# Linear attention and soft mixture of experts on one core: the phases of the loop put in another order, the first pair and the table setup moved between engines

## Chip, core and metric

The kernel runs on one core of one Trainium2 chip. A core has five engines that run side by side, each in its own program order: TensorE (PE, matrix products and transposes[...]; its weight loads are shown as PEld), VectorE (DVE), ScalarE (ACT), GpSimd (POOL[...]) and SyncE (SP, which here only issues transfers). An engine that meets an instruction whose input is not ready waits, and all that stands behind it in that engine's program waits too. The order of instructions in this kernel is the order in which they are written, engine by engine; the framework adds the semaphores. The metric is the time of one execution on the device, in microseconds (us).

## What is computed

Two steps, one after the other. The first is a linear attention with a decaying state, for 4 batches of 8 heads, 768 positions, head size 48. The second is a soft mixture of 8 experts with 4 slots each, on all 3072 rows of 384.

```python
# r, k, v: [4, 8, 768, 48]   w, u: [8, 48]   phi: [384, 32]   w1: [8, 384, 1024]   w2: [8, 1024, 384]
for t in range(S):
    y[:, :, t] = r_t @ (state + (u * k_t) v_t^T)
    state = w * state + k_t v_t^T
x = y as [3072, 384]
logits = x @ phi
d = softmax of logits over the rows;  slot_input = d.T @ x
for e in range(8):
    slot_out[e] = relu(slot_input[e] @ w1[e]) @ w2[e]
out = softmax of logits over the slots @ slot_out
```

## The kernel before

The sequence is cut into chunks of 128 positions. Two chunks make a pair (256 rows), so there are 12 pairs, three to a batch. For a pair `n` the program has these parts (`P` = 128, `J` = 2 interleaved position sets, `H` = 8 heads, `D` = 48, `nP` = 4 head pairs; `g` is the chunk of the pair):

```python
def mults(n):                       # scale r and k by powers of w; u * k; cast v
    nc.gpsimd.tensor_mul(rr[:, :, :, 0:D], jh(r_l), W_n[:])
    nc.gpsimd.tensor_mul(kk[:, :, :, 0:D], jh(k_l), W_k[:])
    nc.gpsimd.tensor_mul(ku[:], jh(k_l), u_rep[...])
    nc.scalar.copy(v_bf[:], jh(v_l))

def r_copy(n, j):                   # r into PSUM, tile rp (one buffer)
    nc.scalar.copy(s["rp"][:], jh(loads[n][0])[:, j, :, :])
def kur(n, j):
    nc.vector.tensor_mul(ku[:, j], ku[:, j], rp[:])
def diag(n):                        # sum of u*k*r per head, times v: the position's own term
    nc.vector.tensor_reduce(d, ku[:], axis=X, op=add)
    nc.vector.tensor_mul(dv[:], v_bf[:], d[...])

def trans(n, nm):                   # eight transposes into t_p (one buffer), then a copy
    nc.tensor.transpose(t_p[...], ...)          # x8
    nc.scalar.copy(t_s[:], t_p[:])

def att(n, j):                      # 16 matmuls into at_p0, at_p1 (one buffer each), then two masks
    nc.tensor.matmul(at_p[a][...], kT[...], rT[...])
    nc.vector.tensor_mul(s["at"][:, j, a, :, :], at_p[a][:], mask[:, j, None, :])

def y_open(n):    ...               # 4 matmuls: dv into y_p
def inter(n, g):  ...               # 4 matmuls: earlier state times r, into y_p
def state(n, g):                    # new state in PSUM s_p (one buffer), then times w^128
    nc.tensor.matmul(s_p[:], ident[:], st[...])
    nc.tensor.matmul(s_p[...], kk[...], v_bf[...])     # x8
    nc.vector.tensor_mul(st2[...], s_p[:], wm[...])
def intra(n):                       # 32 matmuls: masked attention times v; then x copied to SBUF
    nc.tensor.matmul(y_p[...], at_s[...], v_bf[...])
    nc.scalar.copy(x_t[:], y_p[...])

def xt(n):        ...               # 6 transposes of x, copy on ScalarE (xt_s)
def lg(n):        ...               # 6 matmuls: logits; exponential on ScalarE (Lexp)
def disp(n, s_p): ...               # 8 matmuls: d.T @ x and the column sums; added to un_a on VectorE
def lexp_t(g):                      # every second pair: exponentials transposed, row sums
    nc.tensor.transpose(le_p[...], Lexp, ident);  nc.vector.tensor_copy(LexpT[...], le_p[...])
    nc.tensor.matmul(rs_p, LexpT[...], blk);      nc.vector.reciprocal(rsum_r[...], rs_p)

def tables():                       # w^128 by seven squarings; tables for state and logits
    for _ in range(C.bit_length() - 1):
        nc.vector.tensor_mul(w_pd[:], w_pd[:], w_pd[:])
    for par in range(2):
        nc.vector.tensor_copy(wm[...], w_pd[...])
    nc.vector.tensor_copy(phi_s[:], phi_f[:])
```

The start and the loop call them like this:

```python
mults(0); mults(1)
r_copy(0, 0); kur(0, 0); r_copy(0, 1); kur(0, 1)
trans(0, "rr"); trans(0, "kk")
tables()
diag(0)
for n in range(nS + 2):             # nS = 12; calls for pairs that do not exist do nothing
    load(n + 3)
    disp(n - 2, s_now)
    att(n, 0)
    mults(n + 2)
    trans(n + 1, "rr")
    r_copy(n + 1, 0); kur(n + 1, 0)
    att(n, 1)
    trans(n + 1, "kk")
    r_copy(n + 1, 1); kur(n + 1, 1)
    y_open(n); inter(n, 0); state(n, 0)
    xt(n - 1)
    inter(n, 1); state(n, 1); intra(n)
    lg(n - 1)
    diag(n + 1)
    if 2 <= n and n % 2 == 0: lexp_t(n // 2 - 1)
    load_w(W_AT[n])                 # weights of the experts, issued on GpSimd's queue
```

After the loop the column sums are inverted, the experts run (`up`, `down`), and the output is made from `LexpT` and the slot outputs, in 24 blocks written by 12 transfers.

Of the kernel before, what the change touches and what calls it, by code (L numbers as in the profile page):

```python
# [11 lines left out]
def kernel(  # L12
# [52 lines left out]
    def load(n):  # L65
        if n >= nS:
            return
        b, i = divmod(n, nSb)
        loads[n] = []
        for name, src in (("r_l", r), ("k_l", k), ("v_l", v)):  # L70
            t = ld.tile([P, H, J, D], f32, name=name)
            nc.sync.dma_start(out=t[:].rearrange("p h j d -> p h (j d)"),  # L72
                              in_=src[b, :, i * TS:(i + 1) * TS, :].rearrange("h (p j) d -> p h (j d)", j=J))
            loads[n].append(t)

# [5 lines left out]
    u_rep = cst.tile([P, H, D], f32, name="u_rep")  # L81
    nc.scalar.dma_start(out=u_rep[:].rearrange("p h d -> p (h d)"), in_=u.flatten().partition_broadcast(P))
    for n in range(3):
        load(n)

    w_pd = cst.tile([P, nP], f32, name="w_pd")
    nc.vector.memset(w_pd[:], 1.0)
    warm = cst.tile([P, 1], f32, name="warm")
# [7 lines left out]
    make_identity(nc, ident)  # L96
    for par in range(2):
        nc.gpsimd.dma_start(out=w_pd[par * 64:par * 64 + D, :],
                            in_=w.rearrange("(q a) d -> a d q", a=2)[par])
    phi_f = cst.tile([P, nM, ES], f32, name="phi_f")  # L100
# [11 lines left out]
    nc.vector.tensor_copy(col_f[:], col_i[:])  # L112
    mask = cst.tile([P, J, P], f32, name="mask")
    for j in range(J):
# [30 lines left out]
    st_t = [cst.tile([P, nP, D2], bf, name=f"st{i}") for i in range(2)]  # L145

    def tables():
        for _ in range(C.bit_length() - 1):
            nc.vector.tensor_mul(w_pd[:], w_pd[:], w_pd[:])  # L149
        for par in range(2):  # L150
            sl = slice(par * 64, par * 64 + 64)
            nc.vector.tensor_copy(wm[sl, :, par * D:(par + 1) * D],
                                  w_pd[sl, :, None].to_broadcast([64, nP, D]))
        nc.vector.tensor_copy(phi_s[:], phi_f[:])

# [22 lines left out]
    with tc.tile_pool(name="wk", bufs=2) as wk, \  # L178
# [4 lines left out]
        def mults(n):  # L183
            if n >= nS:
                return
            r_l, k_l, v_l = loads[n]
            rr, kk = rr_t[n % NB], kk_t[n % NB]
            nc.gpsimd.tensor_mul(rr[:, :, :, 0:D], jh(r_l), W_n[:])  # L188
            nc.gpsimd.tensor_mul(kk[:, :, :, 0:D], jh(k_l), W_k[:])  # L189
            ku = wk.tile([P, J, H, D], f32, name="ku")  # L190
            nc.gpsimd.tensor_mul(ku[:], jh(k_l), u_rep[:, None, :, :].to_broadcast([P, J, H, D]))  # L191
            v_bf = wk3.tile([P, J, H, D], bf, name="v_bf")
            nc.scalar.copy(v_bf[:], jh(v_l))
            sc[n] = dict(rr=rr, kk=kk, ku=ku, v=v_bf, at={})

# [37 lines left out]
        def att(n, j):  # L233
            if n >= nS:
                return
            s = sc[n]
            rT, kT = s["t_rr"], s["t_kk"]
            if j == 0:
                s["at"] = wk.tile([P, J, 2, nP, P], bf, name="at_s")
            at_p = [ps.tile([P, nP, P], f32, name=f"at_p{a}") for a in range(2)]  # L240
            for q in range(nP):
                for g in range(2):
                    for a in range(2):
                        sl = slice(a * 64, a * 64 + 64)
                        nc.tensor.matmul(at_p[a][g * HF:(g + 1) * HF, q, :], kT[sl, q, g, j, :],  # L245
                                         rT[sl, q, g, :, :].rearrange("p j c -> p (j c)"),
                                         start=True, stop=True, tile_position=(a * 64, g * HF),
                                         skip_group_check=True)
            for a in range(2):
                nc.vector.tensor_mul(s["at"][:, j, a, :, :], at_p[a][:],  # L250
                                     mask[:, j, None, :].to_broadcast([P, nP, P]))
# [24 lines left out]
        def state(n, g):  # L276
# [4 lines left out]
            first = i == 0 and g == 0  # L281
            if g == 0 and "s" not in s:
                s["s"] = ps.tile([P, nP * D2], f32, name="s_p")
            s_p = s["s"]
            st, st2 = st_t[(2 * n + g) % 2], st_t[(2 * n + g + 1) % 2]
            if not first:
# [3 lines left out]
            for q in range(nP):  # L290
                for j in range(J):
# [4 lines left out]
                                     tile_position=(g * HF, 0), skip_group_check=True)  # L296
            nc.vector.tensor_mul(st2[:].rearrange("p q e -> p (q e)"), s_p[:],  # L297
                                 wm[:].rearrange("p q e -> p (q e)"))
# [3 lines left out]
        def intra(n):  # L302
            s = sc[n]
            for a in range(2):
                for q in range(nP):
                    h = 2 * q + a
                    for j in range(J):
                        for g in range(2):
                            sl = slice(g * HF, (g + 1) * HF)
                            nc.tensor.matmul(s["y"][:, g, h * D:(h + 1) * D], s["at"][sl, j, a, q, :],  # L310
                                             s["v"][sl, j, h, :],
                                             start=False, stop=(a == 1 and q == nP - 1 and j == J - 1),
                                             tile_position=(g * HF, 0), skip_group_check=True)
            x_t = wk3.tile([P, 2, Dm], bf, name="x_t")
            nc.scalar.copy(x_t[:], s["y"][:, :, 0:Dm])  # L315
            x_of[n] = x_t
            del sc[n]
# [15 lines left out]

        le_of = {}

        def lg(n):
            if not 0 <= n < nS:
                return
            xl_p, xt_s = xl_of.pop(n)
            lg_p = xl_p[:, XW:XW + 4 * ES].bitcast(f32)  # L340
            for g in range(2):
                for mi in range(nM):
                    o = (g * nM + mi) * P
                    nc.tensor.matmul(lg_p[:, g * ES:(g + 1) * ES], xt_s[:, o:o + P], phi_s[:, mi, :],
                                     start=(mi == 0), stop=(mi == nM - 1), skip_group_check=True)
            if n % 2 == 0:
                le_of[n // 2] = wk.tile([P, G, ES], bf, name="Lexp")
            nc.scalar.activation(out=le_of[n // 2][:, 2 * (n % 2):2 * (n % 2) + 2, :].rearrange("p g s -> p (g s)"),
                                 in_=lg_p, func=AF.Exp)

        def disp(n, s_p):
# [14 lines left out]
            del x_of[n]  # L366

        def lexp_t(g):
            le_p = ps.tile([P, P + 2 * G], bf, name="le_p", tag="xl_p", padded_shape=[P, XW + 4 * ES])
            nc.tensor.transpose(le_p[:, 0:P], le_of[g][:].rearrange("p g s -> p (g s)"), ident[:])  # L370
            nc.vector.tensor_copy(LexpT[:, g, :].rearrange("s (p j) -> s j p", j=J),
                                  le_p[:, 0:P].rearrange("s (j p) -> s j p", j=J))
            rs_p = le_p[:, P:P + 2 * G].bitcast(f32)
            nc.tensor.matmul(rs_p, LexpT[:, g, :], blk[:], start=True, stop=True, skip_group_check=True)
            nc.vector.reciprocal(rsum_r[:, g * G:(g + 1) * G], rs_p)

        W_AT = [0, 1, 1, 1, 1, 1, 1, 1, 1, 1, 1, 2, 2, 2, 2]
        mults(0)
        mults(1)
        r_copy(0, 0)  # L380
        kur(0, 0)
        r_copy(0, 1)
        kur(0, 1)
        trans(0, "rr")
        trans(0, "kk")
        tables()
        diag(0)
        for n in range(nS + 2):
            live = n < nS
            load(n + 3)  # L390
            if live:
                sc[n]["s"] = ps.tile([P, nP * D2], f32, name="s_p")
                s_now = sc[n]["s"]
            else:
                s_now = ps.tile([P, nP * D2], f32, name="s_p")
            disp(n - 2, s_now)
            att(n, 0)
            mults(n + 2)
            trans(n + 1, "rr")
            r_copy(n + 1, 0)  # L400
            kur(n + 1, 0)
            att(n, 1)
            trans(n + 1, "kk")
            r_copy(n + 1, 1)
            kur(n + 1, 1)
            if live:
                y_open(n)
                inter(n, 0)
                state(n, 0)
            xt(n - 1)  # L410
            if live:
                inter(n, 1)
                state(n, 1)
                intra(n)
            lg(n - 1)
            diag(n + 1)
            if 2 <= n and n % 2 == 0 and n // 2 <= nG:
                lexp_t(n // 2 - 1)
            load_w(W_AT[n])
# [93 lines left out]
```

The softmax here doesn't subtract the row's maximum and nothing guards it: scores larger than these inputs give would overflow.

## Time and profile before

The median of two runs is 176.5 us (175.2 and 177.8); the profiled execution has a span of 173.4 us.

| Engine | busy, us | share of the span | instructions |
|---|---|---|---|
| TensorE, matmuls | 108.8 | 63% | 1927 |
| TensorE, weight loads | 80.3 | 46% | 1927 |
| VectorE | 103.3 | 60% | 205 |
| ScalarE | 74.1 | 43% | 114 |
| GpSimd | 81.2 | 47% | 64 |

| What the loop is made of | engine | count | mean, us |
|---|---|---|---|
| rr, kk, ku products (lines 188, 189, 191) | GpSimd | 12 each | 1.84, 1.81, 1.81 |
| mask products, `at_s` (line 250) | VectorE | 48 | 0.68 |
| `ku` times `rp` (line 208) | VectorE | 24 | 0.55 |
| reduce and `dv` (lines 215, 217) | VectorE | 12 each | 0.95, 0.95 |
| state table `st` (line 297) | VectorE | 20 | 0.56 |
| copies `t_rr`, `t_kk` (line 230) | ScalarE | 12 each | 1.01 |
| copies `xt_s`, `x_t`, cast `v_bf` | ScalarE | 12 each | 0.80, 0.80, 0.83 |
| copy `rp` (line 202) | ScalarE | 24 | 0.49 |

The page of a profile gives the busy time of each engine; then the span in 40 equal slices, each digit being a busy share in tenths (the row PEclk is the granted clock of TensorE in tenths); then the groups of instructions with what ended the idle time before them. A line of the timeline has start, duration (both us), engine, source line, operation, output and inputs, shapes and count, and in brackets the idle time of that engine just ahead, with the instruction that ended it. A line of the windows has the stretch, its length, busy us and number of instructions for PE, PEld, DVE, ACT and POOL, then granted clock, DMA share and GB/s. Busy time of TensorE is modelled at the end of each matmul, since matmuls are pipelined.

### The profile page before, as it was taken

How to read it: one execution, taken by the hardware profiler on the slowest of the kernel's cores; microseconds unless marked ns; L12 is line 12 of the kernel's file. 1: busy time of each engine (PE TensorE's matmuls, PEld its weight loads, DVE VectorE, ACT ScalarE, POOL GpSimd, SP SyncE). 2: the span in 40 equal slices, each digit the busy share in tenths (PEclk: the TensorE clock that was granted, in tenths of full speed). 3: DMA queues.
4: the chain of work that ended last, by engine and by line, in shares of the span. 5: the costliest groups of instructions: out<-in, count | busy, mean ns of one | idle time of the engine just before them, and what ended most of it. 6: DMA issues, size and time to landing. Idle time of an engine off the chain costs nothing.

```text
span 173.4 us, 4471 instructions
## 1 busy us (share of the span) xinstructions
PE 108.8 (63%) x1927; PEld 80.3 (46%) x1927; DVE 103.3 (60%) x205; ACT 74.1 (43%) x114; POOL 81.2 (47%) x64
## 2 busy tenths in 40 slices
PE   0020505679567889598748979797984838978200
PEld 0010403556445566466536756565663628962000
DVE  2062999394895686668775587666766333328510
ACT  3534521265765546547743555463550320008510
POOL 7089948193999085776758096991000000000000
PEclk9999999999995555857985555555576575555555
DMA  5999980559999997989999909299999993005994
GB/s 66 252 278 308 319 241 0 132 144 161 292 145 293 218 262 107 271 143 215 241 242 197 146 4 146 43 166 210 208 207 210 205 206 49 8 4 203 365 363 160
DMA packets 52628, 32.19 MB, mean 186 GB/s; under 512 B 38000, under 2 KB 49520, under 8 KB 52608
## 3 DMA queue, kind: packets, MB, share of 16 engines
q0 software_dynamic: 11616, 12.63, 46.2%
q1 hardware_dynamic: 40848, 19.07, 38.5%
q10 hardware_dynamic: 144, 0.20, 0.9%
q8 instruction: 15, 0.25, 0.5%
q14 instruction: 5, 0.04, 0.1%
HBM read 39.77 MB, written 4.72 MB: 257 GB/s over the span
## 4 chain that ended last, share of the span: by engine, by line
PE 44%; DVE 22%; ACT 14%; DMA 7%; SPq 5%; issue 4%; ACTq 0%; DVEq 0%
PE t_p L227 10%; PE s_p L292 6%; SPq L72 5%; PE at_p L245 4%; DMA out_dram<-o_s 4%; ACT t_rr L230 4%; PE y_p L272 4%; DVE w_pd L149 4%; DVE at_s L250 4%; DVE dv L217 3%; PE xl_p L329 3%; ACT x_t L315 3%; PE so_p L447 3%; DVE rp L215 3%; PE h_p L435 3%
## 5 line engine op out<-in xcount | busy, mean ns | idle before, releaser
L189 POOL TENSOR_TENSOR kk<-k_l,W_k 128x768 bf16<-128x768 f32 x12 | 21.7, 1808 | 27.3 <-PE s_p L292 27.3
L250 DVE TENSOR_TENSOR at_s<-at_p,mask 128x512 bf16<-128x512 f32 x48 | 30.8, 684 | 2.6 <-PE at_p L245 2.4
L245 PE MATMUL at_p<-t_rr,t_kk 64*64 64x128 bf16 x384 | 17.8, 294 | 12.8 <-DVE at_s L250 11.7
L208 DVE TENSOR_TENSOR ku<-ku,rp 128x384 f32<-128x384 f32 x24 | 13.3, 554 | 19.8 <-ACT rp L202 19.6
L188 POOL TENSOR_TENSOR rr<-r_l,W_n 128x768 bf16<-128x768 f32 x12 | 22.1, 1843 | 5.5 <-DVE W_n L125 5.3
L191 POOL TENSOR_TENSOR ku<-k_l,u_rep 128x768 f32<-128x768 f32 x12 | 21.7, 1812 | 2.8 <-DVE rp L215 2.8
L230 ACT COPY t_rr<-t_p 128x1024 bf16<-128x1024 bf16 x12 | 12.1, 1012 | 16.6 <-PE t_p L227 16.5
L245 PEld LDWEIGHTS <-t_kk 64*64 64x64 bf16 x384 | 11.0, 145 | 17.3 <-issue 15.3
L227 PE MATMUL t_p<-ident,rr 128*128 128x128 bf16 x96 | 11.6, 296 | 11.5 <-POOL rr L188 11.5
L297 DVE TENSOR_TENSOR st<-s_p,wm 128x384 bf16<-128x384 f32 x20 | 11.1, 556 | 11.4 <-PE s_p L292 11.4
L230 ACT COPY t_kk<-t_p 128x1024 bf16<-128x1024 bf16 x12 | 12.1, 1012 | 11.8 <-PE t_p L227 11.8
L331 ACT COPY xt_s<-xl_p 128x768 bf16<-128x768 bf16 x12 | 9.6, 800 | 17.0 <-PE xl_p L329 17.0
L227 PE MATMUL t_p<-ident,kk 128*128 128x128 bf16 x96 | 11.4, 294 | 6.1 <-ACT t_rr L230 5.4
L315 ACT CAST x_t<-y_p 128x768 bf16<-128x768 f32 x12 | 9.6, 799 | 13.2 <-PE y_p L310 13.2
L227 PEld LDWEIGHTS <-rr 128*128 128x128 bf16 x96 | 8.6, 135 | 13.2 <-POOL rr L188 11.5
L292 PE MATMUL s_p<-v_bf,kk 64*128 64x96 bf16 x160 | 14.5, 254 | 0.0
L480 ACT ACTIVATE o_s<-o_p,rsum_r 128x384 f32<-128x384 f32 x12 | 6.4, 585 | 18.1 <-PE o_p L474 15.6
L202 ACT COPY rp<-r_l 128x384 f32<-128x384 f32 x24 | 11.7, 488 | 5.1 <-DVE dv L217 4.4
L292 PEld LDWEIGHTS <-kk 64*128 64x128 bf16 x160 | 10.7, 121 | 6.4 <-issue 6.4
L176 POOL DMA_DIRECT2D w_all<-in_moe_w_dram x16 | 13.6, 856 | 0.0
L227 PEld LDWEIGHTS <-kk 128*128 128x128 bf16 x96 | 9.2, 132 | 7.8 <-issue 6.1
L272 PE MATMUL y_p<-st,t_rr 128*128 128x96 bf16 x80 | 8.9, 254 | 5.0 <-DVE st L297 5.0
(76 smaller groups left out, 185.7 us busy)
## 6 DMA issues: line engine op xcount, KB each, us to landing
w_all<-in_moe_w_dram POOLq DMA_DIRECT2D x16, 768.0 KB, 8.5
r_l<-in_r_dram SPq DMA_DIRECT2D x12, 384.0 KB, 4.9
k_l<-in_k_dram SPq DMA_DIRECT2D x12, 384.0 KB, 5.4
v_l<-in_v_dram SPq DMA_DIRECT2D x12, 384.0 KB, 6.4
out_dram<-o_s SPq DMA_DIRECT2D x12, 384.0 KB, 4.2
w_rep<-in_w_dram SPq DMA_DIRECT2D x1, 192.0 KB, 5.5
u_rep<-in_u_dram ACTq DMA_DIRECT2D x1, 192.0 KB, 6.0
phi_f<-in_moe_phi_dram POOLq DMA_DIRECT2D x1, 48.0 KB, 6.4
```

Of the source, the lines that this page charges most:

```text
L176: nc.gpsimd.dma_start(out=dst[:, e, :, :], in_=src[:, e, :, :])
L188: nc.gpsimd.tensor_mul(rr[:, :, :, 0:D], jh(r_l), W_n[:])
L189: nc.gpsimd.tensor_mul(kk[:, :, :, 0:D], jh(k_l), W_k[:])
L191: nc.gpsimd.tensor_mul(ku[:], jh(k_l), u_rep[:, None, :, :].to_broadcast([P, J, H, D]))
L208: nc.vector.tensor_mul(s["ku"][:, j, :, :], s["ku"][:, j, :, :], s["rp"][:])
L227: nc.tensor.transpose(t_p[:, q, :, j, :], s[nm][:, j, 2 * q:2 * q + 2, :].rearrange("p h d -> p (h d)"), ident[:])
L230: nc.scalar.copy(t_s[:], t_p[:])
L245: nc.tensor.matmul(at_p[a][g * HF:(g + 1) * HF, q, :], kT[sl, q, g, j, :], rT[sl, q, g, :, :].rearrange("p j c -> p (j c)"), start=True, s ...
L250: nc.vector.tensor_mul(s["at"][:, j, a, :, :], at_p[a][:], mask[:, j, None, :].to_broadcast([P, nP, P]))
L272: nc.tensor.matmul(s["y"][:, g, q * D2:(q + 1) * D2], s["t_rr"][:, q, g, :, :].rearrange("p j c -> p (j c)"), st[:, q, :], start=False, st ...
L292: nc.tensor.matmul(s_p[:, q * D2:(q + 1) * D2], s["kk"][sl, j, 2 * q:2 * q + 2, :].rearrange("p h d -> p (h d)"), s["v"][sl, j, 2 * q:2 * ...
L315: nc.scalar.copy(x_t[:], s["y"][:, :, 0:Dm])
```

## The change

It moves work between engines at the start and reorders the loop; the arithmetic of the result stays. What it is for:

- Start: the seven squarings of `w_pd` go from VectorE to GpSimd, and the three table copies from VectorE to ScalarE, so that VectorE is free for the first pair. The small transfers of `w_pd` are issued on ScalarE's queue, ahead of the loads of the first pair; `k` is loaded before `r`, with `u` behind it.
- The first pair is scaled on VectorE; GpSimd makes only its `ku`. The second pair is scaled after the first pair's setup.
- The mask is bf16 in place of fp32, and the masked attention is stored with its two indices exchanged.
- In the loop `att(n, 0)` goes ahead of the dispatch, so that it lies in the wait for the exponential; `att(n, 1)` comes behind the transposes of `rr`, with the masks directly behind each half.
- The product that makes the next state table, the cast of `v`, the copy of x, the exponential and the row sums become calls of their own: the state table of chunk 0 goes ahead of the second `r_copy`, that of chunk 1 behind `diag`.
- Routing (`lexp_t`, row sums) comes one pair later, in the middle of the round, and its copy goes from VectorE to ScalarE.
- The first expert weights are issued one round earlier.

```diff
-        for name, src in (("r_l", r), ("k_l", k), ("v_l", v)):
+        for x, src in ((1, k), (0, r), (2, v)):
 ...
+            if n == 0 and x == 1:
+                nc.sync.dma_start(out=u_rep[...], in_=u...)
-    nc.scalar.dma_start(out=u_rep[...], in_=u...)
+    for par in range(2):
+        nc.scalar.dma_start(out=w_pd[par * 64:par * 64 + D, :], in_=w...)
-    for par in range(2):
-        nc.gpsimd.dma_start(out=w_pd[par * 64:par * 64 + D, :], in_=w...)
-    mask = cst.tile([P, J, P], f32, name="mask")
+    mask = cst.tile([P, J, P], bf, name="mask")
+    for _ in range(C.bit_length() - 1):
+        nc.gpsimd.tensor_mul(w_pd[:], w_pd[:], w_pd[:])
     def tables():
-        for _ in range(C.bit_length() - 1):
-            nc.vector.tensor_mul(w_pd[:], w_pd[:], w_pd[:])
         for par in range(2):
-            nc.vector.tensor_copy(wm[...], w_pd[...])
-        nc.vector.tensor_copy(phi_s[:], phi_f[:])
+            nc.scalar.copy(wm[...], w_pd[...])
+        nc.scalar.copy(phi_s[:], phi_f[:])
 ...                                                # mults(n)
+            if n == 0:
+                nc.gpsimd.tensor_mul(ku[:], jh(k_l), u_b)
+                nc.vector.tensor_mul(rr[:, :, :, 0:D], jh(r_l), W_n[:])
+                nc.vector.tensor_mul(kk[:, :, :, 0:D], jh(k_l), W_k[:])
+            else:                                   # as before, on GpSimd
 ...                                                # lexp_t, rowsum
-            nc.vector.tensor_copy(LexpT[...], le_p[...])
+            nc.scalar.copy(LexpT[...], le_p[...])
-        W_AT = [0, 1, 1, 1, 1, 1, 1, 1, 1, 1, 1, 2, 2, 2, 2]
+        W_AT = [1, 1, 1, 1, 1, 1, 1, 1, 1, 1, 2, 2, 1, 1]
```

The start and the loop after the change:

```python
mults(0)
trans(0, "rr"); r_copy(0, 0); trans(0, "kk")
v_cast(0)
tables()
kur(0, 0); r_copy(0, 1); kur(0, 1)
diag(0)
mults(1)
for n in range(nS + 2):
    load(n + 3)
    group = (n - 3) // 2 if n >= 3 and n % 2 == 1 else None
    att(n, 0)
    mults(n + 2)
    disp(n - 2, s_now)
    trans(n + 1, "rr")
    att(n, 1)
    r_copy(n + 1, 0); kur(n + 1, 0)
    if group is not None: lexp_t(group)
    y_open(n); inter(n, 0); state(n, 0)
    st_next(n, 0)
    r_copy(n + 1, 1); kur(n + 1, 1)
    v_cast(n + 1)
    trans(n + 1, "kk")
    if group is not None: rowsum(group)
    xt(n - 1)
    inter(n, 1); state(n, 1)
    diag(n + 1)
    st_next(n, 1)
    intra(n)
    x_copy(n)
    lg(n - 1)
    expo(n - 1)
    load_w(W_AT[n])
```

## The prediction

> **What bounds the kernel now.** I read the page first: busy shares, then the slices of the span.
>
> ```profile
> PE 108.8 (63%) x1927; PEld 80.3 (46%) x1927; DVE 103.3 (60%) x205; ACT 74.1 (43%) x114; POOL 81.2 (47%) x64
> ...
> PEclk9999999999995555857985555555576575555555
> ```
>
> No engine is full, so stages must be read one by one. There are four: start (0 to 27 us), 12 loop rounds (to about 132), drain (to 143.5), experts and output (to 173.4; the change leaves these two alone). Second, VectorE's (DVE) timeline of the start, then TensorE's (PE):
>
> ```profile
> 17.01 0.56 DVE L208 TENSOR_TENSOR ku<-ku,rp 128x384 f32<-128x384 f32 x1 [0.55 <-ACT rp L202]
> 17.48 6.95 DVE L149 TENSOR_TENSOR w_pd<-w_pd 128x4 f32<-128x4 f32 x7
> ...
> 25.13 0.95 DVE L215 TENSOR_REDUCE rp<-ku 128x16 f32<-128x768 f32 x1
> 26.12 0.95 DVE L217 TENSOR_TENSOR dv<-v_bf,rp 128x768 bf16<-128x768 bf16 x1
> 26.99 1.28 DVE L250 TENSOR_TENSOR at_s<-at_p,mask 128x512 bf16<-128x512 f32 x2
> ```
>
> ```profile
> 20.08 0.64 PE L245 MATMUL at_p<-t_rr,t_kk 64*64 64x128 bf16 x16 [1.10 <-ACT t_kk L230]
> 20.66 1.03 PE L227 MATMUL t_p<-ident,rr 128*128 128x128 bf16 x8
> 27.73 0.26 PE L245 MATMUL at_p<-t_rr,t_kk 64*64 64x128 bf16 x1 [6.04 <-DVE at_s L250]
> ```
>
> Seven squarings of a 128x4 table take 6.95 us, and the first masks stand behind them: TensorE sits idle for 6.04 us. The tile view says how far one squaring varies:
>
> ```profile
> L149 DVE TENSOR_TENSOR w_pd<-w_pd x7: 161/1061/1739, 17.5 to 24.3; 128x4 f32<-128x4 f32 x7
> ```
>
> Third, the loop, by windows laid on its rounds (PE busy, PEld, DVE, ACT, POOL, then granted clock):
>
> ```profile
> 44.70:53.30 8.60, 5.41 (x127) 4.00 (x123) 7.18 (x13) 5.65 (x9) 8.18 (x7) 0.95 1.03 211
> ...
> 91.50:101.40 9.90, 8.89 (x134) 6.52 (x130) 6.32 (x12) 4.85 (x8) 5.16 (x5) 0.50 0.80 135
> 101.40:111.10 9.70, 8.28 (x127) 5.93 (x123) 7.04 (x13) 5.63 (x9) 8.13 (x6) 0.50 0.50 83
> 111.10:121.00 9.90, 8.26 (x130) 6.15 (x127) 6.32 (x12) 4.52 (x7) 6.46 (x8) 0.50 1.00 160
> ```
>
> At clock 0.5 TensorE works 8.3 to 8.9 us of 9.7 to 9.9, so it is nearly the bound; at clock 1 it works 5.4 of 8.6, and VectorE (7.2) is the busiest engine that nothing frees. Where TensorE's holes are, its timeline shows:
>
> ```profile
> 101.12 0.24 PE L359 MATMUL s_p<-Lexp,x_t 128*128 128x32 bf16 x3 [0.73 <-ACT Lexp L348]
> ...
> 103.46 0.64 PE L245 MATMUL at_p<-t_rr,t_kk 64*64 64x128 bf16 x15 [0.18 <-DVE at_s L250]
> ```
>
> 0.73 us at the head of each round (x copy, exponential, then dispatch) and about 0.4 before the second attention half, whose PSUM waits for the masks. Rounds with a group transpose add LexpT (waits of 0.74 and 0.40 us), and a round that opens a batch waits 0.63 us for the state table.
>
> **The Trainium skill.** "SBUF — State Buffer", section Who interferes with whom: a VectorE instruction with two SBUF inputs contends with a GpSimd instruction that reads SBUF, and whoever came first keeps the port. The trace agrees: squarings take 161 ns with GpSimd idle and up to 1739 while it multiplies (1795 ns each); `ku x rp`, with one input in PSUM, keeps 0.55 us throughout. "TensorE: Matmul & The Clock Gate", Part 1: the clock is either half or full, decided per window of about 3.4 us by how busy TensorE was. The trace agrees: changes lie at 52.5, 69.6, 73.0, 79.8, 90.1, 127.6 us, multiples of 3.41 apart. Windows that lost the clock had 1.66 to 1.82 us of TensorE work, windows that kept it 2.35 to 2.64, and only wholly filled half-clock windows won it. (Before 42 us the page's "9" is not real: eight transposes take 1.03 us at 28.9, against 0.62 at 45.) "VectorE: DVE Perf Modes", Why PSUM operands drop a tier: with an fp32 PSUM input no faster mode. So the bf16 mask should leave 684 ns as it is; no run here shows it yet.
>
> **The change part by part.**
>
> *Squarings to GpSimd, table copies to ScalarE (ACT).* VectorE loses 6.95 + 0.52 + 0.21 = 7.7 us before the first masks. GpSimd gains seven 128x4 products, about 0.2 us each (estimate from VectorE's free 161 ns), behind the landing of `w_pd` (6.8 to 7.4 us after issue now). Issued first on ScalarE's queue, it lands by 8.2 at worst; squarings end near 9.6. ScalarE gains about 0.85 us (two copies of 192, one of 96 elements; estimate from 0.48 us for 384).
>
> *First pair scaled on VectorE.* Two products of 768 elements at about 0.95 us (as `dv`), both with two SBUF inputs, so GpSimd may hold them up. `W_k` ends at 9.8, memsets at 11.7 as now; rr(0) 11.7 to 12.7, transposes to 13.7, ScalarE's copy to 14.8, rp to 15.3; kk(0) by 13.6 to 14.5; its transposes 15.0 to 16.0, copy to 17.1. The v cast (0.83) and the tables (0.85) follow on ScalarE to 18.8, second rp 19.3, ku x rp 19.9, reduce 20.8, dv 21.8. First masks at 21.8 in place of 27.0. The removed 7.7 us does not come back whole, for the chain through ScalarE is longer.
>
> *Round 0.* From the masks on: masks 1.3, second attention half 0.6, y 0.5, first state 0.75, then chain state table 0.56, rp, ku, reduce, dv (VectorE now takes the second state table behind `diag`), second state product and intra. I get attention of round 1 at 29.3; before it starts at 34.6 by the timeline. Gain **5.3**.
>
> *Loop.* At half clock rounds hold 8.42 us of TensorE work (mean of 8.26, 8.89, 8.28, 8.26) in 9.85, so 1.43 of holes. Attention (0.57) now stands ahead of dispatch, so of 0.73 only 0.2 is left; dispatch (0.38) stands between the attention halves with the transposes, so the masks (0.2 + 1.29 after attention) end as the transposes end: 0.4 falls to about 0.1; the state table is ahead of the last ku product, so the 0.63 of every third round goes; LexpT's two waits lie beside other matmuls. Remaining holes about 0.4: **8.8** a round.
> At full clock TensorE needs 5.4. The chain is attention 0.35, masks to 1.83, attention 2.3, masks to 3.8, ku to 4.35, rp 4.9, v cast 5.75, kk copy 6.7, xt copy 7.5, logits 7.9: **8.0**, against 8.6 and 9.4 before. VectorE's 7.2 minus LexpT fits inside.
> The clock: TensorE at half clock will stand almost without a hole from dispatch to logits, some 8 us, so a filled window occurs in most rounds, and the clock is won more often; at full clock work is 5.4/8.0 of the time, 2.3 us a window, above the 1.8 that lost, but the window around intra and logits comes to about 1.85, so it falls again. I take 45% full: 0.55 x 8.8 + 0.45 x 8.0 = 8.44, and 8.6 with something for waits I do not see. Before, ten rounds from 34.6 to 131.5: 9.69 each. Gain 10 x (9.69 - 8.6) = **10.9**.
>
> *Drain.* Dispatch of the last pair goes ahead of the last group transpose (0.64 gained), but VectorE then takes the group's reciprocal ahead of the column sum (about the same lost): **0**.
>
> Sum: 176.5 - 5.3 - 10.9 = 160.3; I say **161**.
>
> **Rivals.** (1) *GpSimd's port* gives the start back: if each of the two VectorE products waits a whole GpSimd product (1.8), first masks come 2 to 3 us later, total 163.5. For: squarings at 1739 ns. Against: kk(0) has slack until 15.0. (2) *Weights become the bound.* The last eight weights are issued in a burst at 110.8 and fill the DMA at 207 GB/s until about 143.5: 4.1 us each. After, nine are issued before the burst, which starts near round 9 (about 100), so seven end near 129, plus at most one in hand: 133. Experts start near 129 and need the last about 9 us later. Against it, but by few us; it would cap the time near 158. (3) *Clock.* Always half: the loop gains 8.9, total 163; always full: 16.9, total 154. (4) *VectorE's new order binds*: state table behind `diag` delays the next round's state; then rounds stay at 9.3 and the total is 167.
>
> **Range and chances.** Rivals give 154 to 167, and I allow more on the slow side for chains I missed: 154 to 169. Under 173 counts as faster by 2%: 0.94; within 2% 0.04; slower 0.02. All removed waits stand on the chain that ends last, and nothing is added but about 1 us on ScalarE.
>
> **What would show it.** Right: first masks at 21 to 23 us; squarings on GpSimd well below 0.5 us each; no idle over 2 us before the second attention half of round 0; dispatch waiting under 0.3 us; rounds of 8.3 to 8.9; the mask product still at 0.68 us; more full-clock slices; VectorE's rr(0), kk(0) between 0.9 and 2.7 us. Wrong: rounds above 9.3, DMA named as releaser before experts' matmuls, or `st` waiting behind `diag` with TensorE idle.

## Result, and the profile after

The changed kernel takes 147.6 us (147.3 and 147.9) against 176.5: ratio 0.836, 95% interval 0.809 to 0.864. The prediction was 161, with a range from 154 to 169: the direction is right and the size is outside the range. The interval is wide because each kernel ran twice; the experiments have more executions, and their ratios refer to executions of the kernel before on the same chip.

The page of the kernel after, busy shares and clock:

```profile
span 145.3 us, 4488 instructions
...
PE 95.6 (66%) x1927; PEld 73.2 (50%) x1927; DVE 96.0 (66%) x191; ACT 75.4 (52%) x123; POOL 77.9 (54%) x67
...
PEclk9999999999995559999975589555995555555555
```

The 1927 matmuls are the same, but TensorE is busy for 95.6 us in place of 108.8: more of them run at the full clock. VectorE lost 7.3 us: the squarings, tables and `LexpT` copies left it, and the two products of the first pair came. No engine is full.

The start, VectorE's timeline of the kernel after (start, duration, and in brackets the idle time before):

```profile
7.18 0.56 DVE L125 TENSOR_TENSOR W_n<-W_n,w_rep 128x384 f32<-128x384 f32 x1 [4.81 <-ACT W_n L123]
...
10.06 1.64 DVE L192 TENSOR_TENSOR rr<-r_l,W_n 128x768 bf16<-128x768 f32 x1
11.63 0.95 DVE L193 TENSOR_TENSOR kk<-k_l,W_k 128x768 bf16<-128x768 f32 x1
...
20.47 1.28 DVE L261 TENSOR_TENSOR at_s<-at_p,mask 128x512 bf16<-128x512 f32 x2
```

The first masks start at 20.47, where 26.99 stood before. Beside GpSimd's `ku`, `rr` takes 1.64 us, and 0.95 is what the equal `kk` takes without it. The squarings, by the tile view of `w_pd`, and TensorE's wait before the second attention half of round 0:

```profile
L148 POOL TENSOR_TENSOR w_pd<-w_pd x7: 196/198/521, 6.7 to 8.9; 128x4 f32<-128x4 f32 x7
```

```profile
21.21 0.26 PE L256 MATMUL at_p<-t_rr,t_kk 64*64 64x128 bf16 x1 [3.59 <-DVE at_s L261]
21.80 0.64 PE L256 MATMUL at_p<-t_rr,t_kk 64*64 64x128 bf16 x15 [0.34 <-DVE at_s L261]
```

Seven squarings end by 9.1, and 3.59 us of idle time remain of 6.04. The loop, by windows laid from one first mask to the next (columns as before):

```profile
58.56:65.75 7.19, 5.12 (x123) 4.00 (x124) 6.21 (x11) 5.32 (x10) 7.17 (x5) 1.00 1.19 258
65.75:72.94 7.19, 4.88 (x125) 3.75 (x124) 6.64 (x11) 5.08 (x9) 5.23 (x5) 1.00 1.19 241
72.94:82.05 9.11, 8.40 (x132) 6.42 (x133) 6.78 (x12) 5.61 (x10) 5.48 (x4) 0.58 1.17 238
```

A round at full clock takes 7.19 us where TensorE works 5; one mostly at half clock takes 9.1, and TensorE is nearly the bound. GpSimd (the fifth engine of the line) is busy for 7.17 us of the first of these rounds and for 5.23 of the second, and both take 7.19 us, so it does not set their length. The head of a round in TensorE's timeline:

```profile
58.10 0.42 PE L256 MATMUL at_p<-t_rr,t_kk 64*64 64x128 bf16 x16
58.68 0.23 PE L381 MATMUL s_p<-Lexp,x_t 128*128 128x32 bf16 x3 [0.16 <-ACT Lexp L370]
...
59.90 0.41 PE L256 MATMUL at_p<-t_rr,t_kk 64*64 64x128 bf16 x15 [0.25 <-DVE at_s L261]
```

Dispatch waits 0.16 us in place of 0.73. And VectorE's timeline over one round:

```profile
69.21 0.55 DVE L310 TENSOR_TENSOR st<-s_p,wm 128x384 bf16<-128x384 f32 x1
69.84 0.56 DVE L219 TENSOR_TENSOR ku<-ku,rp 128x384 f32<-128x384 f32 x1
70.43 0.96 DVE L226 TENSOR_REDUCE rp<-ku 128x16 f32<-128x768 f32 x1
71.50 0.95 DVE L228 TENSOR_TENSOR dv<-v_bf,rp 128x768 bf16<-128x768 bf16 x1
72.37 0.55 DVE L310 TENSOR_TENSOR st<-s_p,wm 128x384 bf16<-128x384 f32 x1
72.94 1.29 DVE L261 TENSOR_TENSOR at_s<-at_p,mask 128x512 bf16<-128x512 f32 x2
```

Reduce and `dv` (diag) run while TensorE makes the second state product, so the second `st` finds it ready. Where the time went, by the start of the first masks of a round in both traces: round 1 begins at 27.77 (before 36.39), so the start gave 8.6 us; ten rounds take 77.6 (before 95.8), the loop gave 18.2; from the last round's masks to the end 39.9 (before 41.2), 1.3. The sum, 28.1, is the difference of the spans.

### The profile page after: what moved, and what is told of

It is laid out like the page before. It is cut to its first block, busy times and chain, and to the rows that moved or that the text cites. A ratio compares the mean times of both kernels' runs of the same rounds, so it can differ in the third digit from the quotient of the medians.

```text
span 145.3 us, 4488 instructions
## 1 busy us (share of the span) xinstructions
PE 95.6 (66%) x1927; PEld 73.2 (50%) x1927; DVE 96.0 (66%) x191; ACT 75.4 (52%) x123; POOL 77.9 (54%) x67
## 4 chain that ended last, share of the span: by engine, by line
PE 34%; DVE 22%; ACT 19%; DMA 13%; issue 7%; SPq 0%; ACTq 0%; DVEq 0%
DVE at_s L261 11%; PE at_p L256 6%; DMA out_dram<-o_s 5%; DMA r_l<-in_r_dram 5%; ACT t_kk L241 4%; DVE ku L219 4%; PE t_p L238 4%; PE h_p L470 4%; ACT xt_s L346 4%; PE so_p L482 4%; PE xl_p L344 3%; PE s_p L301 3%; ACT v_bf L204 3%; DMA w_rep<-in_w_dram 3%; ACT x_t L330 2%
## 5 line engine op out<-in xcount | busy, mean ns | idle before, releaser
L196 POOL TENSOR_TENSOR kk<-k_l,W_k 128x768 bf16<-128x768 f32 x11 | 19.9, 1810 | 11.3 <-PE s_p L301 10.7
L195 POOL TENSOR_TENSOR rr<-r_l,W_n 128x768 bf16<-128x768 f32 x11 | 20.0, 1821 | 1.9 <-DVE kk L193 1.7
L197 POOL TENSOR_TENSOR ku<-k_l,u_rep 128x768 f32<-128x768 f32 x11 | 20.0, 1816 | 0.0
L256 PE MATMUL at_p<-t_rr,t_kk 64*64 64x128 bf16 x384 | 15.0, 264 | 7.3 <-DVE at_s L261 6.2
L238 PE MATMUL t_p<-ident,rr 128*128 128x128 bf16 x96 | 9.8, 263 | 11.8 <-DVE rr L192 11.8
L515 ACT ACTIVATE o_s<-o_p,rsum_r 128x384 f32<-128x384 f32 x12 | 6.4, 585 | 16.3 <-PE o_p L509 13.8
L256 PEld LDWEIGHTS <-t_kk 64*64 64x64 bf16 x384 | 9.3, 128 | 10.7 <-issue 8.1
L238 PEld LDWEIGHTS <-rr 128*128 128x128 bf16 x96 | 7.3, 118 | 12.1 <-DVE rr L192 11.8
L228 DVE TENSOR_TENSOR dv<-v_bf,rp 128x768 bf16<-128x768 bf16 x12 | 11.4, 954 | 1.2
L226 DVE TENSOR_REDUCE rp<-ku 128x16 f32<-128x768 f32 x12 | 11.5, 958 | 0.3
L238 PE MATMUL t_p<-ident,kk 128*128 128x128 bf16 x96 | 9.9, 265 | 1.1 <-ACT t_rr L241 1.1
```

The costliest lines, as they stand in the source:

```text
L197: nc.gpsimd.tensor_mul(ku[:], jh(k_l), u_b)
L238: nc.tensor.transpose(t_p[:, q, :, j, :], s[nm][:, j, 2 * q:2 * q + 2, :].rearrange("p h d -> p (h d)"), ident[:])
```

## Experiments

Ratios are to the kernel before, with 95% intervals. "Round" is the mean over ten rounds, first masks to first masks: 9.58 us before (9.69 in the prediction, which counted from attention), 7.76 after. The letters of the theories are those of the texts on record. Executions of one kernel fall into faster and slower ones; medians are of all, ratios of the faster ones alone, and the traces of `att_first_only` and `st0_late` show slower ones, so no times are read from these two.

### Start and loop apart

**start_only**: the kernel before with the start of the kernel after.

```diff
 # kernel before; squarings on GpSimd, tables on ScalarE, first pair on VectorE, order of loads
-mults(0); mults(1)
-r_copy(0, 0); kur(0, 0); r_copy(0, 1); kur(0, 1)
-trans(0, "rr"); trans(0, "kk"); tables(); diag(0)
+mults(0); trans(0, "rr"); r_copy(0, 0); trans(0, "kk"); v_cast(0); tables()
+kur(0, 0); r_copy(0, 1); kur(0, 1); diag(0); mults(1)
```

> The kernel before with only the start of the changed one (load order, w_pd squarings on GpSimd, tables on ScalarE, first pair scaled on VectorE); its loop stays in the old order. If start and loop add up, the 7.7 us that the traces show up to the attention of round 1 are gained and nothing more: 168. If the start also shifts the clock or the DMA in the loop: below 164 or above 171.

170.7 us, ratio 0.959 (0.951 to 0.967). First masks at 20.23, but rounds still 9.78. The start alone is worth 4.1%, 7.2 us.

**loop_only**: the loop of the kernel after behind the start of the kernel before (the reverse edit).

> The changed kernel with the start of the one before (the complement of start_only). If start and loop add up: 147.6 plus the 7.2 us that start_only gained, 154 to 156. If the new loop hides part of the late start: 150 to 153.

153.8 us, 0.874 (0.868 to 0.880); first masks at 26.84, rounds 7.69. The loop alone gives 12.6%, 22.2 us of 176.5. With 7.2 from the start that is 29.4; measured 28.9. The two add, within the intervals, and three quarters lie in the loop.

### Moves added to the loop of before

**masks_only**: `r_copy` and `kur` of chunk 0 behind `att(n, 1)`.

```diff
-    r_copy(n + 1, 0); kur(n + 1, 0)
     att(n, 1)
+    r_copy(n + 1, 0); kur(n + 1, 0)
```

> The kernel before with one move: the first r copy and the ku product of the next pair go behind the second attention half, so that VectorE has all four masks without a wait for ScalarE between them. Theory A (VectorE's program order held the masks, and with them TensorE and the clock): 8 us faster, about 167. Theory B (the hole at the head of the round, before dispatch, was what cost): at most 2 us, 173 or more.

177.5 us, 1.010 (1.004 to 1.016): no gain, if anything slightly slower. Theory A falls. VectorE's timeline of this kernel shows what stands ahead of the masks:

```profile
101.32 0.56 DVE L297 TENSOR_TENSOR st<-s_p,wm 128x384 bf16<-128x384 f32 x1 [1.64 <-PE s_p L292]
101.79 0.95 DVE L215 TENSOR_REDUCE rp<-ku 128x16 f32<-128x768 f32 x1
102.78 0.95 DVE L217 TENSOR_TENSOR dv<-v_bf,rp 128x768 bf16<-128x768 bf16 x1
103.65 0.28 DVE L365 TENSOR_TENSOR un_a<-un_a,s_p 128x128 f32<-128x128 f32 x1
103.93 0.69 DVE L250 TENSOR_TENSOR at_s<-at_p,mask 128x512 bf16<-128x512 f32 x1
```

VectorE waits 1.64 us for the second state product, and only then come reduce, `dv` and the masks.

**att_first_only**: the first attention half ahead of dispatch.

```diff
+    att(n, 0)
     disp(n - 2, s_now)
-    att(n, 0)
```

> The kernel before with one move: the first attention half ahead of dispatch. Theory B (the masks' start is what the round waits for, and the wait for the exponential and the dispatch stood ahead of it): about 1 us in each of 10 rounds, 8 to 11 us faster, 166 to 169. Theory D (this order pays only together with the other moves, for the old loop has later waits that take its place): at most 3 us faster, 174 or more.

174.2 us, 0.995 (0.991 to 0.999), about 0.9 us.

**diag_only**: VectorE's reduce and `dv` ahead of the second state table.

```diff
     state(n, 1)                 # matmuls only
+    diag(n + 1); st_next(n, 1)
     intra(n); lg(n - 1)
-    diag(n + 1)
```

> The kernel before with one move: reduce and dv of the next pair ahead of the second state table on VectorE. Theory E (the next masks are held by two chains side by side: VectorE's wait for the state product with state table, reduce and dv behind it, and TensorE's wait for the exponential with dispatch ahead of the attention; undoing one leaves the other): at most 3 us faster, 173 or more. If this chain alone held the masks: 8 us or more, below 169.

174.0 us, 0.987 (0.983 to 0.992), about 2.2 us. `st` now waits 0.5 us in all for the state product, 11.4 before, yet little is gained.

**pair_only**: both of these moves.

> The kernel before with both moves, attention ahead of dispatch and reduce and dv ahead of the second state table, and nothing else of the change. Theory E: far more than the sum of the two alone, 9 to 14 us faster, 163 to 168. Theory D (more of the change is needed): at most 5 us faster, 171 or more.

169.2 us, 0.965 (0.958 to 0.973), 6.1 us: twice 0.9 and 2.2 together, and between the two ranges expected: theory E is right in kind, and too large in size. Two chains run side by side at the round's end. On TensorE: logits, exponential, dispatch, attention. On VectorE: state product, state table, reduce, `dv`, masks. Freeing one leaves the other to end last.

**pair_masks**: the pair, and the masks directly behind as in `masks_only`.

> The kernel before with three moves: attention ahead of dispatch, reduce and dv ahead of the second state table, and the first r copy and ku product behind the second attention half. Theory E, carried on (once the pair is undone the next wait to end is VectorE's for the r copy, 1.23 us a round in the pair's trace): 3 to 6 us faster than the pair, 163 to 166. Theory H (TensorE's own work at half clock is the bound by now): within 1.5 us of the pair, 168 to 171.

168.4 us, 0.958 (0.950 to 0.966); rounds 9.17, as in `pair_only` (9.16). The waits of VectorE for `rp` fall from 21.6 to 15.8 us without moving the round, so they were not the bound, and H's number came out. TensorE's own work was not the bound for long, though: the next two steps gain another 14 us with the same matmuls. A wait that the kernel before had only in its start sits in most rounds since `pair_only`; TensorE's timeline of `pair_masks`:

```profile
82.41 0.70 PE L245 MATMUL at_p<-t_rr,t_kk 64*64 64x128 bf16 x16
83.63 1.01 PE L227 MATMUL t_p<-ident,kk 128*128 128x128 bf16 x8 [0.53 <-ACT t_rr L230]
```

The transposes of `kk` write the single buffer that ScalarE still copies `rr` out of.

**plus_st0**: `pair_masks`, and the first state table ahead of the second `r_copy` and `kur`.

```diff
     trans(n + 1, "kk")
-    r_copy(n + 1, 1); kur(n + 1, 1)
     y_open(n); inter(n, 0); state(n, 0)
+    r_copy(n + 1, 1); kur(n + 1, 1)
```

> The loop with attention ahead of dispatch, masks directly behind it and VectorE's diag ahead of the second state table, and now also the first state table ahead of the second r copy and ku product. Without the last step it took 168.4 us (ratio 0.958). Theory L (the moves of the loop add up in this order as they came out when undone alone: 3.5 us for this one): 163 to 166 us. Theory M (the step only pays once the kk transposes stand later, because TensorE still waits for the copy of rr ahead of them, 9.0 us in all): 167 us or more.

165.5 us, 0.932 (0.922 to 0.942); rounds 8.83. 2.6% more, 4.5 us, inside theory L's range. Theory M expected no gain here (167 or more), and that part of it falls.

**plus_st0_kk**: and the `kk` transposes behind both.

```diff
-    trans(n + 1, "kk")
     y_open(n); inter(n, 0); state(n, 0)
     r_copy(n + 1, 1); kur(n + 1, 1)
+    trans(n + 1, "kk")
```

> The same, with the kk transposes also moved behind the first state product, as in the kernel after; only routing and the separate cast of v are still as before. The kernel with all of the loop's moves and the old start took 153.8 us. Theory L: 4 us from kk and 3.5 from the state table, 159 to 162 us, and routing with its copy off VectorE and the cast of v bring the rest. Theory M: kk is the move that frees the others, 154 to 158 us, PE's wait for the copy of rr (9.0 us) falls under 3 us, and GpSimd's wait for the buffer of kk (25.5 us) falls under 15 us. Theory N (routing and the cast of v carry the rest): 164 us or more.

155.4 us, 0.877 (0.867 to 0.886); rounds 7.76, exactly those of the kernel after. This step brings 5.6%, 9.8 us; the number is theory M's, although M's reason had failed one step before, and N falls. M's waits held only in part: GpSimd's wait for the buffer of `kk` falls from 20.7 to 13.8 us, and of TensorE's wait for the copy of `rr` 5.8 us remain, all in the start. In the loop `plus_st0` had 9.0 less 5.9 of the start: 3.1 us. So more than the wait came back. The page rows of the clock, first `plus_st0`, then `plus_st0_kk`:

```profile
PEclk9999999999997556855555589555555555555555
```

```profile
PEclk9999999999998579955985799559977655555555
```

At 45 to 125 us the mean granted clock is 0.60 and 0.78. What goes with it stands in TensorE's timeline. A half-clock round of `plus_st0` works without a hole from 70.79 to 76.5 us, then waits 0.17 for the exponential; one of `plus_st0_kk` works from 80.40 to 88.4:

```profile
70.79 1.01 PE L227 MATMUL t_p<-ident,kk 128*128 128x128 bf16 x8 [0.32 <-ACT t_rr L230]
...
76.67 0.24 PE L366 MATMUL s_p<-Lexp,x_t 128*128 128x32 bf16 x3 [0.17 <-ACT Lexp L355]
```

```profile
80.40 0.64 PE L245 MATMUL at_p<-t_rr,t_kk 64*64 64x128 bf16 x16
...
85.65 0.80 PE L336 MATMUL xl_p<-ident,x_t 128*128 128x128 bf16 x6
86.29 0.33 PE L272 MATMUL y_p<-st,t_rr 128*128 128x96 bf16 x4
...
88.64 0.23 PE L366 MATMUL s_p<-Lexp,x_t 128*128 128x32 bf16 x3 [0.25 <-ACT Lexp L355]
```

No bracket stands between 80.40 and 88.64, and the same four matmuls that take 0.48 to 0.50 at half clock take 0.33 from 86.29 on. The clock is decided in windows of 3.41 us, as the Trainium skill says ("TensorE: Matmul & The Clock Gate", Part 1) and the change times in the prediction show. In `plus_st0_kk` the window from 82.84 to 86.26 lies wholly inside the stretch, and the clock rises behind it. But the stretch of `plus_st0` holds a whole window too, 71.55 to 74.96 with TensorE busy throughout, and the clock stays at half until 95.4. So longer stretches go with more full clock here, but a filled window alone does not explain it, and what decides stays open. That the clock carries the 6.7 us beyond the wait is argued, not measured by itself.

What `loop_only` has beyond this kernel (routing one pair later with its copy on ScalarE, cast of `v` and copy of x apart, bf16 mask, earlier weights) changes 0.877 to 0.874: nothing measurable. The ladder, in us of 176.5 by the ratios: the pair 6.1, masks 1.3 (inside the noise), first state table 4.5, `kk` 9.8, the rest 0.4, the start 6.7; together 28.8.

### Moves undone one at a time in the kernel after

The losses given are differences of the medians to 147.6 us. By the ratios they are, in the order below, 11.3, 15.3, 6.7, 4.2, 3.8, 1.1 and 4.6 us, and the interval of the kernel after alone is ±4.8 us, so the small ones are not certain.

**disp_first**: dispatch ahead of attention again.

```diff
+    disp(n - 2, s_now)
     att(n, 0); mults(n + 2)
-    disp(n - 2, s_now)
```

> The changed kernel with dispatch ahead of the first attention half again, as before. Theory B: 0.7 us of wait back in each of 12 rounds, 6 to 8 us slower, about 155. Theory A: the wait only moves, for VectorE is what a full-clock round waits for: up to 3 us slower, 148 to 151.

159.3 us, 0.900 (0.893 to 0.908): 11.7 us lost, more than either theory expected, by one move that gains 0.9 alone. TensorE's timeline of this kernel has the old hole of the round's head again:

```profile
61.95 0.23 PE L381 MATMUL s_p<-Lexp,x_t 128*128 128x32 bf16 x3 [0.76 <-ACT Lexp L370]
...
62.23 0.42 PE L256 MATMUL at_p<-t_rr,t_kk 64*64 64x128 bf16 x16
```

**st_old**: both state tables in VectorE's old order.

```diff
     y_open(n); inter(n, 0); state(n, 0)
-    st_next(n, 0)
     r_copy(n + 1, 1); kur(n + 1, 1)
+    st_next(n, 0)
 ...
     inter(n, 1); state(n, 1)
-    diag(n + 1); st_next(n, 1)
+    st_next(n, 1); diag(n + 1)
```

> The changed kernel with the two state tables in VectorE's old order (behind the second ku product; ahead of the reduce). Theory B: 0 to 3 us slower, 148 to 151. Theory D: 5 us or more slower, 153 or more.

161.0 us, 0.923 (0.916 to 0.930): 13.4 us lost, the most of any edit, as theory D expected. VectorE's timeline has the order of before, wait and all:

```profile
80.79 0.56 DVE L310 TENSOR_TENSOR st<-s_p,wm 128x384 bf16<-128x384 f32 x1 [1.64 <-PE s_p L301]
81.27 0.95 DVE L226 TENSOR_REDUCE rp<-ku 128x16 f32<-128x768 f32 x1
82.32 0.95 DVE L228 TENSOR_TENSOR dv<-v_bf,rp 128x768 bf16<-128x768 bf16 x1
83.19 1.28 DVE L261 TENSOR_TENSOR at_s<-at_p,mask 128x512 bf16<-128x512 f32 x2
```

**diag_late** and **st0_late**: its two halves, the second state table ahead of diag, and the first one behind the second `kur`.

> The changed kernel with only the second state table ahead of reduce and dv again. Theory E: nearly all that the old state order cost, 157 to 161. Theory F (the first state table, ahead of the second ku product, is what counted): at most 3 us slower, 148 to 151.

> The changed kernel with only the first state table behind the second ku product again. Theory E: at most 2 us slower, 147 to 150. Theory F: 8 us or more slower.

153.4 us, 0.875 (0.864 to 0.885), and 151.1 us, 0.860 (0.851 to 0.870): 5.8 and 3.5 us lost, together 9.3 of 13.4. So they seem to hide for each other in part; `diag_late` came out below theory E's range and above F's, `st0_late` above E's and below F's.

**kk_early**: the `kk` transposes directly behind the second attention half, `r_copy` and `kur`.

> The changed kernel with the kk transposes directly behind the second attention half again, ahead of y, inter and state, their copy ahead of the second r copy on ScalarE. Theory B: within 2 us of 148. Theory D: 4 us or more slower, since the state table then comes 0.6 to 1 us later in each round.

151.8 us, 0.858 (0.850 to 0.865), single times from 149.9 to 157.0: 4.2 us lost by a median that two long times raise, less than the 9.8 that the move brings in `plus_st0_kk`. Holes of 0.31 to 0.86 us ahead of these transposes are back.

**masks_late**: `r_copy` and `kur` of chunk 0 ahead of `att(n, 1)` again.

> The changed kernel with that one move undone. Theory A: 8 us slower, about 155, and VectorE waits for the r copy again in each round. Theory B: at most 2 us slower, below 150.

149.8 us, 0.842 (0.837 to 0.848): 2.1 us lost.

**routing_old**: `lexp_t` and row sums at the round's end, copy on VectorE.

> The changed kernel with the group transposes, their copy on VectorE and the row sums at the end of every second round again, ahead of the next attention. Theory B: the waits of LexpT (0.7 + 0.4 us in six rounds) stand ahead of the attention again: 5 to 7 us slower, about 154. Theory D: the same or less.

150.6 us, 0.862 (0.856 to 0.868): 2.9 us lost by the medians, although `plus_st0_kk` and `loop_only`, which differ in it too, are equal: a loss of this size is not certain.

### What binds now

**vcast_early**: the kernel after, the cast of `v` ahead of the second `r_copy`.

```diff
+    v_cast(n + 1)
     r_copy(n + 1, 1); kur(n + 1, 1)
-    v_cast(n + 1)
     trans(n + 1, "kk")
```

> The changed kernel with the cast of v ahead of the second r copy on ScalarE, into its wait for the ku product. Theory G (a round at full clock is bound by VectorE, busy 6.2 to 6.8 of 7.2 us): 1 to 2.5 us faster, 145 to 147. If the chain over ScalarE (r copy, v cast, kk copy, xt copy, logits) binds: 0.8 us a round, 5 to 8 us faster, 140 to 143.

145.7 us, 0.831 (0.822 to 0.839): the lowest ratio, though its interval overlaps that of the kernel after. The total lies in theory G's range by luck, for the rounds say otherwise: 7.18 in place of 7.76, and at full clock down to 6.54 in place of 7.19. So the chain over ScalarE did bind them (0.8 us a round was expected of it). ScalarE's timeline of the kernel after shows what it shortens:

```profile
62.13 0.48 ACT L213 COPY rp<-r_l 128x384 f32<-128x384 f32 x1 [0.92 <-DVE ku L219]
62.55 0.83 ACT L204 CAST v_bf<-v_l 128x768 bf16<-128x768 f32 x1
63.29 1.00 ACT L241 COPY t_kk<-t_p 128x1024 bf16<-128x1024 bf16 x1
64.19 0.80 ACT L346 COPY xt_s<-xl_p 128x768 bf16<-128x768 bf16 x1
64.88 0.81 ACT L330 CAST x_t<-y_p 128x768 bf16<-128x768 f32 x1
```

After 0.92 us of idle time ScalarE stands without a hole until the logits can start; the cast fits into that hole. Yet of the 5.8 us (ten times 0.58) only 1.9 reach the median, and 3.5 the span of the two traces. In its trace GpSimd waits 8.4 us for loads of `r` (DMA), and TensorE stops in the middle of the experts:

```profile
117.22 0.19 PE L482 MATMUL so_p<-hT,w_all 128*128 128x4 bf16 x2
119.01 0.73 PE L482 MATMUL so_p<-hT,w_all 128*128 128x4 bf16 x22 [1.59 <-issue]
```

Its windows show the transfers at 188 GB/s until 118.5, with 57 in the half us after it. The trace names no releaser, but the weights are the only stream left, so they are the likely one.

**warm_after**: the kernel after with extra work, eight spare matmuls of 128 columns behind `intra`, so that TensorE keeps its clock.

```diff
     intra(n)
+    for _ in range(8):
+        nc.tensor.matmul(y_p[...], ident[:], ones[:])   # into unused columns
     x_copy(n)
```

> The changed kernel with eight spare 128-column matmuls into unused PSUM columns behind intra, where TensorE waits for the xt copy at full clock. If the clock is what is left (full-clock rounds 7.2 to 7.4 us, half-clock ones 8.5 to 9.1) and the spare work holds it: 3 to 5 us faster, 143 to 145. If it does not hold the clock: their own time at half clock, 0.9 us in some rounds, 1 to 5 us slower.

148.9 us, 0.847 (0.841 to 0.854), not the gain expected. The clock from 45 to 105 us is 0.94 in place of 0.76, and rounds take 7.54 in place of 7.76: 2.2 us of gain in the loop. They are gone before the experts start (116.9; after 116.8), for the clock is 0.51 from 105 to 117, against 0.65 in the kernel after; then comes the same stop as in `vcast_early`, 1.71 us. The full-clock rounds take 7.19 us with and without the spare work. In this loop the steadier clock is worth 0.2 us a round.

## Why the prediction missed

The predicted gain was 16.2 us and the spans differ by 28.1. Of the 11.9 us between, the loop has 7.3, the start 3.3 and the end 1.3.

- **Removed holes, the mechanism: right.** Dispatch waits 0.16 us ("under 0.3"), first masks at 20.47 (0.5 us ahead of "21 to 23"), no DMA releaser ahead of the experts, mask product 686 ns against 684: the bf16 mask does nothing, as "VectorE: DVE Perf Modes" had it. Squarings 198 ns, estimate 0.2.
- **Start, 5.3 us: too small.** Measured 7.2 alone, and attention of round 1 at 26.87 where 29.3 was worked out. 1.54 us of it: the product `W_n` starts at 7.18 and not at 8.72 as in the kernel before, because `w_rep` has landed and is used at 4.69 in place of 6.24 with the new order of issues (all traces with the new start have `W_n` at 7.07 to 7.21, all with the old one at 8.40 to 8.99). The prediction kept "as now" for a part that the change also touches. GpSimd's port (rival 1) cost 0.69 us once. "No idle over 2 us" in round 0 was wrong: 3.59.
- **Loop, 8.6 us a round: the failed step.** Measured 7.76. The half-clock term was right (8.8; the three rounds with dispatch and the clock at 0.57 to 0.62 take 8.51, 8.74 and 9.11). The term that was mis-sized is the chain of a full-clock round: **8.0** predicted, and 7.19 in the three that are wholly at full clock. The chain was the right one, from attention over masks, `ku`, `rp`, cast, `kk` and `xt` to the logits: `vcast_early` takes the cast out of it, and such rounds fall to 6.54. But the durations of the groups were added. In the round whose attention starts at 58.10, `ku` starts 3.46 us later (3.8 worked out), the copy of `kk` 5.19 (5.75), that of `xt` 6.09 (6.7) and the next attention 7.19 (8.0). Starts of neighbours lie closer than a duration: in ScalarE's lines above 0.83 takes 0.74, 1.00 takes 0.90, 0.80 takes 0.69. VectorE's `ku` and TensorE's next attention:

```profile
61.56 0.54 DVE L219 TENSOR_TENSOR ku<-ku,rp 128x384 f32<-128x384 f32 x1
...
65.29 0.42 PE L256 MATMUL at_p<-t_rr,t_kk 64*64 64x128 bf16 x16
```

- **Clock, 45%: its price was wrong too.** Full clock was granted in 53% of the time of the ten rounds (up to 33.4 us the row shows 9, but eight transposes take 1.03 us at 31.5, so that stretch counts as half). But losing it in part costs little: the three rounds with the clock at 0.75 to 0.83 take 7.42 to 7.45 us, as in this window:

```profile
82.05:89.47 7.42, 5.59 (x121) 4.32 (x121) 6.17 (x10) 5.09 (x9) 7.40 (x6) 0.83 0.85 149
```

  Together with the first, which has no dispatch (7.40), seven of ten rounds have about the full-clock length, mean 7.32. By length, the miss of 0.84 a round splits into 0.45 x (8.0 - 7.32) = 0.31, 0.25 x (8.79 - 7.32) = 0.37, and the 0.16 "for waits I do not see", which were not there. The windows that the share rested on do not sort this kernel: those that lost the clock had 1.89 to 2.59 us of TensorE work, those that kept it 2.27 to 3.0; two of four gains came behind windows of 3.24 us of work, and the wholly filled one from 74.4 to 77.8 brought none.
- **Rival 4 had its sign wrong.** The state table behind diag was taken as a risk. It removes VectorE's wait (1.64 us in the lines of `masks_only`) from the chain to the masks, and undoing the order of state tables costs 13.4 us. The 11.4 us of `st` waits stood in the waits of before and were not read.
- **The move of `kk` has no term in the sum.** Before, other waits hid its hole; with these gone it would have been the new wait, and the change had already put it away. It is the largest step of the ladder.
- **Experts and output, taken as unchanged:** 1.3 us with the drain (0 predicted).
- **Rival 2**, the weights, did not bind here, but very likely does in `vcast_early`. GpSimd, busy for 8.18 of 8.60 us in the prediction's first window, was no rival there, and did not bind either.

What stays open: what decides the clock, and why `kk` and routing weigh 9.8 and 0.4 when added last but 4.2 and 2.9 when undone; noise may be part of the second.

## To carry to other kernels

Where two engines' chains end side by side, moves tried alone mislead: 0.9 and 2.2 us alone, 6.1 together, while undoing a single one in the finished kernel cost up to 11.7. Judge a reordering on the whole, and for each hole removed ask which wait it has been hiding. Build a chain from the spacing of starts in the timeline, not from mean durations.

## What the hardware showed beyond that

- One VectorE product of 768 elements with two SBUF inputs took 1.64 us beside GpSimd and 0.95 without; the Trainium skill ("SBUF — State Buffer", Who interferes with whom) has the cause, and the 0.69 us added were less than a whole GpSimd product (1.81).
- The row PEclk can show 9 up to the first recorded change though the clock is half: in `masks_only`, with its first change at 71.3 us, eight transposes take 1.03 us at 65.3 under a 9, and 0.62 at 84.1, where full clock is on record from 81.5 on. Read a share of clock only behind the first change.
- A higher clock is not itself a gain: `warm_after` ran the stretch from 45 to 105 us at 0.94 (after 0.76) and was no faster.
- Starts of neighbours on ScalarE lay 0.06 to 0.11 us closer than the duration of the first in the timeline shown for `vcast_early`'s reading.
